# The last three output products by seven block products instead of eight

## The chip, the cores and the metric

The kernel runs on one core of a Trainium2 chip. It uses the core's five engines, which run side by side and meet only at semaphores: TensorE (PE in the profile, with its weight loads as PEld), VectorE (DVE), ScalarE (ACT), GpSimd (POOL) and SyncE (SP). The metric is the device time of one execution in microseconds. Before the change it is 248.94 us, the median of three runs from 248.42 to 251.67.

## The reference

The program is a linear attention followed by a multiplicative feed-forward network (FFN). There are 8 batches, 8 heads, 576 positions and a head width of 64; the FFN has 4608 tokens (all batches and positions), width 512 and inner width 1024.

```python
q_p = phi(q, cos_w, sin_w)                  # max(x, 0) times cos and sin, concatenated: 128 features
k_p = phi(k, cos_w, sin_w)
kv  = einsum('bhsf,bhsd->bhfd', k_p, v)
num = einsum('bhsf,bhfd->bhsd', q_p, kv)
den = einsum('bhsf,bhf->bhs', q_p, sum(k_p, axis=2)) + 1e-06
x   = (num / den) as [4608, 512]            # heads side by side
h   = ((x @ w1) * (x @ w2)) @ w3            # [4608, 1024]
out = h @ w_out                             # [4608, 512], float32
```

The kernel multiplies w3 and w_out together once, into `w34b` (1024 x 512, bf16), so that a token's output is `((x @ w1) * (x @ w2)) @ w34b`.

## The kernel before, in words

The FFN works on nine tiles of 512 tokens (`ffn_groups(t)`, t from 0 to 8). For each of eight blocks `jc` of the inner width it makes two products of four matmuls of 512 columns, `x @ w1` and `x @ w2` (line 655). ScalarE copies the first out of its PSUM bank as `asb` (line 693), and VectorE multiplies it with the second into `abT[:, jc, :]` (line 698), which lies with the inner width on the partitions and the tokens along the row. Then four output products (one for each 128 tokens, `ms`) take eight matmuls of 512 columns each, with a slice of `abT` as the stationary operand and `w34b[:, jc, :]` as the moving one (line 703). ScalarE copies each to an output buffer (line 709). In the last tile the fourth of them is made in two halves of 256 columns (line 720), which ScalarE and VectorE evict (line 722) and SP stores. The FFN's PSUM banks are four, in rotation, so a bank comes back after three further products.

Outputs go in pairs: an output buffer `osb` holds 256 tokens by 512 columns of float32 (0.52 MB). The list `held` has the pairs that are computed and not yet stored; `st` issues the store of the oldest (line 643) from POOL, `sg` does so behind a one-element copy that waits for the newest `asb` (the copy `seen`, line 415), `sx` behind one that waits for the newest transpose. A pair goes out in two to four DMAs of 128 or 256 KB, or one of 512 KB.

Attention feeds the FFN. For batch b and block c of 128 positions (block 4 has 64): `q b c` and `k b c` make the features (lines 491, 495 and 498, on VectorE and ScalarE), `v b c` copies v (line 510, with V, A or G for VectorE, ScalarE or GpSimd), `qd b c` has SP transpose the features of q by DMA into `qpT` (line 518), `kv b` makes the 40 matmuls of k by v (line 539) and the copies `kvs`, `n b c` eight matmuls of `qpT` by `kvs` into a PSUM pair `pnum` (line 571), `d b c` the division on VectorE (lines 582 to 584, the result is `xblk`), and `xd b c` has SP transpose it by DMA into `xT` of its FFN tile (line 604). Tile 7 needs batch 6's blocks 1 to 4 and batch 7's block 4; tile 8 needs batch 7's blocks 0 to 3. `pnum` has two pairs of banks in turn.

The order of the work on every engine is written out by hand: `PLAN` is a text, a line for each step `f t` of an FFN tile (half of a `jc` pair, or half of an output product) with the attention steps, loads and stores that are issued after it. Each engine runs its instructions in that order, and waits only where a semaphore says so. Loads of q, k and v are issued by POOL (`l`, or `lg` and `lt` behind a `seen` copy), in its own order.

Of the kernel before, what the change touches and what calls it, by code (L numbers as in the profile page):

```python
# [81 lines left out]
f 1  # L82
f 1
f 1; qd 2 3; q 3 2; q 3 3; n 2 2
f 1; k 3 4; k 3 2 4; n 2 4; v 3 0 G
f 1; xd 2 0; xd 2 1; d 2 2
f 1
f 1; v 3 4 G; k 3 0; k 3 3 6; k 3 1; q 3 4 6
f 1; n 2 3; qd 3 0; qd 3 3; xd 2 2
f 1; d 2 4; lt 4 k 0; d 2 3  # L90
f 1; kv 3
f 2
f 2; lg 4 q 0
# [102 lines left out]
f 6; qd 7 2  # L196
f 6; d 6 3; qd 7 4; v 7 4 V; q 7 1
f 6; v 7 1 V
f 6
f 6  # L200
f 6; kv 7; qd 7 0; sg
f 6
f 6; xd 6 1; qd 7 3
f 6
f 6; n 7 4
f 6
f 6
f 6; n 7 3; d 7 4
f 6; n 7 2; xd 6 3
f 6; xd 7 4  # L210
f 6
f 7; d 7 3; qd 7 1
f 7
f 7; n 7 0; xd 7 3
f 7; d 7 2
f 7; d 7 0; xd 7 2
f 7; xd 7 0
f 7; n 7 1
f 7
f 7; d 7 1  # L220
f 7; xd 7 1
f 7
f 7; sx
f 7; st
f 7; st
f 7; sg
f 7
f 7; sg
f 7
f 7  # L230
f 7
f 7
f 7
f 7
f 7; st
f 8
f 8
f 8
f 8
f 8; st  # L240
f 8
f 8
f 8
# [12 lines left out]
f 8  # L256
f 8
f 8
f 8; st; st; st; st; st"""
NKP, NVA, NQP, NRQ, NRV, NT3 = 1, 2, 1, 2, 2, 3  # L260


# [49 lines left out]
def kernel(  # L312
# [34 lines left out]
    osbs = [early[:, ds(2048 * i, 2048)].bitcast(FP32).rearrange("p (i m) -> p i m", m=DM) for i in range(6)]  # L347
# [4 lines left out]
    def osb_of(i):  # L352

        return osbs[i % len(osbs)]
# [166 lines left out]
    pairs, taken = [ps_att], [0]  # L521
# [6 lines left out]
    def second_pair():  # L528

        ps_tr_stack.close()  # L530
        pairs.append(ctx.enter_context(tc.tile_pool(name="ps_att2", bufs=1, side="right", reuse_waits="tile",
                                                    space=bass.MemoryType.PSUM)))

    def kv(b):
        a = att_of(b)
# [109 lines left out]
    def ffn_tile():  # L645

        return ffn_pool[0].tile([P, 512], FP32, name="ffnps")

    def ffn_groups(t):
        x = xT[t]  # L650
        abT = fsb.tile([P, 8, 512], BF16, name="abT", bufs=2)

        def products(out, w, jc, tok):
            for kc in range(4):
                nc.tensor.matmul(out, lhsT=w[:, kc, ts(jc, 128)], rhs=x[:, kc, tok],  # L655
                                 start=(kc == 0), stop=(kc == 3))

        def on_half(half):

            for pair in range(2):  # L660
                a, b = ffn_tile(), ffn_tile()
                if pair == 0:
                    for quarter in range(2):
                        for i in range(2):
                            for ps, w in ((a, w1b), (b, w2b)):
                                products(ps[:, ds(256 * i + 128 * quarter, 128)], w, i,
                                         ds(256 * half + 128 * quarter, 128))
                            if half == 0 and quarter == 0 and i == 0:
# [15 lines left out]
                yield  # L684

        if t <= 1:
            yield from on_half(0)
            yield from on_half(1)
        for jc in range(4 if t <= 1 else 0, 8):
            aT = ffn_tile()  # L690
            products(aT[:, :], w1b, jc, slice(0, 512))
            asb = fsb.tile([P, 512], BF16, name="asb")
            nc.scalar.copy(out=asb[:], in_=aT[:, :])  # L693
            newest[0] = asb
            yield
            bT = ffn_tile()
            products(bT[:, :], w2b, jc, slice(0, 512))
            nc.vector.tensor_mul(out=abT[:, jc, :], in0=asb[:], in1=bT[:, :])  # L698
            yield
        for ms in range(3 if t == NT - 1 else 4):  # L700
            ops = ffn_tile()
            for jc in range(8):
                nc.tensor.matmul(ops[:, :], lhsT=abT[:, jc, ts(ms, 128)], rhs=w34b[:, jc, :],  # L703
                                 start=(jc == 0), stop=(jc == 7))
                if jc == 3:
                    yield
            if ms % 2 == 0:
                osb = osb_of(2 * t + ms // 2)
            nc.scalar.copy(out=osb[:, ms % 2, :], in_=ops[:, :])  # L709
            if t == NT - 1:  # L710
                store(nc.sync, osb[:, ms % 2:ms % 2 + 1, :], 4 * t + ms, 1)
            elif ms % 2 == 1:
                held.append((osb, 4 * t + ms - 1))
            yield
        if t == NT - 1:
            for half in range(2):
                cols = ts(half, 256)
                ops = ffn_tile()
                for jc in range(8):
                    nc.tensor.matmul(ops[:, 0:256], lhsT=abT[:, jc, ts(3, 128)],  # L720
                                     rhs=w34b[:, jc, cols], start=(jc == 0), stop=(jc == 7))
                (nc.vector.tensor_copy if half else nc.scalar.copy)(out=osb[:, 1, cols], in_=ops[:, 0:256])
                store((nc.sync, nc.scalar), osb[:, 1:2, :], 4 * t + 3, 1, cols)
                yield

    def store_next():
        osb, g = held.pop(0)
# [54 lines left out]
    def behind_first_x(c):  # L784

        if c in att[0]["x"]:
            gate(att[0]["x"][c][:, 0, 0, 0:1])

    def gated_store():

        gate(newest[0][:, 0:1])
        store_next()

    def store_behind_transposes():
# [13 lines left out]
        "d": norm, "xt": x_tr, "xd": x_dma, "idle": idle_mms, "open": open_ffn, "second": second_pair,  # L808
        "clear": clear_rows, "t3": w3_tr, "st": store_next,
        "sg": gated_store, "sx": store_behind_transposes,  # L810
    }
    for line in PLAN.splitlines():
# [34 lines left out]
```

## Time and profile before

| what | before |
|---|---|
| median of three runs | 248.94 us |
| the profiled execution: span, first to last instruction | 245.8 us |
| around the span (median less span) | 3.1 us |
| TensorE busy | 238.9 us, 1891 matmuls |
| VectorE busy | 147.9 us, 373 instructions |
| ScalarE busy | 118.5 us, 210 instructions |
| GpSimd busy | 88.9 us, 171 instructions |

The page of the profile gives the span of the profiled execution and not its whole time, so the span is compared with the median of the runs. A row of the timeline has the start in the span, the duration, the engine, the line of the kernel, the operation, what it writes and reads, and in brackets how long its engine was idle before it and what ended that. A busy TensorE is not TensorE at its peak, because matmuls are pipelined: what one of them costs is the distance between their starts, not the duration of one.

### The profile page before, as it was taken

How to read it: one execution, taken by the hardware profiler on the slowest of the kernel's cores; microseconds unless marked ns; L12 is line 12 of the kernel's file. 1: busy time of each engine (PE TensorE's matmuls, PEld its weight loads, DVE VectorE, ACT ScalarE, POOL GpSimd, SP SyncE). 2: the span in 40 equal slices, each digit the busy share in tenths (PEclk: the TensorE clock that was granted, in tenths of full speed). 3: DMA queues.
4: the chain of work that ended last, by engine and by line, in shares of the span. 5: the costliest groups of instructions: out<-in, count | busy, mean ns of one | idle time of the engine just before them, and what ended most of it. 6: DMA issues, size and time to landing. Idle time of an engine off the chain costs nothing.

```text
span 245.8 us, 5011 instructions
## 1 busy us (share of the span) xinstructions
PE 238.9 (97%) x1891; PEld 129.9 (53%) x1891; DVE 147.9 (60%) x373; ACT 118.5 (48%) x210; POOL 88.9 (36%) x171
## 2 busy tenths in 40 slices
PE   8899999989999999999999999999999999999994
PEld 3589434567964545445544544454545454444442
DVE  6976558968888546925855576378458327403320
ACT  2834323767756734755466436558343333323321
POOL 8854887534403170006124023024001000497800
PEclk9999999999999999999999999999999999999999
DMA  7999999999999999879999999999337332489933
GB/s 198 195 196 199 195 177 191 199 199 168 165 163 167 182 135 195 129 138 153 193 138 148 168 144 159 234 148 185 75 61 148 96 75 44 68 267 338 302 119 128
DMA packets 84552, 40.44 MB, mean 165 GB/s; under 512 B 48048, under 2 KB 82096, under 8 KB 84528
## 3 DMA queue, kind: packets, MB, share of 16 engines
q0 software_dynamic: 38832, 27.27, 69.3%
q1 hardware_dynamic: 45696, 12.85, 32.6%
q8 instruction: 15, 0.25, 0.4%
q14 instruction: 9, 0.07, 0.1%
HBM read 38.80 MB, written 9.44 MB: 196 GB/s over the span
## 4 chain that ended last, share of the span: by engine, by line
PE 77%; DMA 9%; POOL 6%; DVE 4%; issue 1%; DVEq 0%; POOLq 0%
PE ffnps L655 45%; PE ffnps L703 24%; DMA early<-in_moe_w_out_dram 4%; PE pnum L571 4%; PE pnum L539 3%; POOL early L403 3%; DMA kf<-in_k_dram 3%; DMA q<-in_q_dram 2%; DVE w3T L460 1%; POOL w2b L776 1%; POOL early L409 1%; DVE kp L491 1%; POOL w1b L776 1%; PE ffnps L720 1%; DVE qp L491 1%
## 5 line engine op out<-in xcount | busy, mean ns | idle before, releaser
L698 DVE TENSOR_TENSOR abT<-asb,ffnps 128x512 bf16<-128x512 bf16 x64 | 43.7, 685 | 56.8 <-PE ffnps L655 56.4
L655 PE MATMUL ffnps<-xT,w1b 128*128 128x512 bf16 (+2 forms) x352 | 76.0, 340 | 0.0
L655 PE MATMUL ffnps<-xT,w2b 128*128 128x512 bf16 (+2 forms) x352 | 76.0, 340 | 0.0
L693 ACT CAST asb<-ffnps 128x512 bf16<-128x512 f32 x64 | 37.4, 584 | 58.6 <-PE ffnps L655 45.5
L703 PE MATMUL ffnps<-w34b,abT 128*128 128x512 bf16 x280 | 65.0, 379 | 0.0
L655 PEld LDWEIGHTS <-w1b 128*128 128x128 bf16 x352 | 31.7, 98 | 28.4
L655 PEld LDWEIGHTS <-w2b 128*128 128x128 bf16 x352 | 31.6, 98 | 28.0
L703 PEld LDWEIGHTS <-abT 128*128 128x128 bf16 x280 | 26.2, 98 | 28.9
L584 DVE TENSOR_TENSOR xblk<-pnum,den 128x512 bf16<-128x512 f32 (+1 forms) x39 | 26.9, 691 | 1.5 <-DVE den L583 0.2
L415 POOL COPY seen<-asb 128x1 bf16<-128x1 bf16 x13 | 2.6, 198 | 50.5 <-ACT asb L693 50.4
L495 ACT ACTIVATE kp<-kf,sinv 128x512 bf16<-128x512 bf16 (+4 forms) x33 | 20.7, 656 | 0.3 <-DMA kf<-in_k_dram 0.3
L495 ACT ACTIVATE qp<-qs,sinv 128x512 bf16<-128x512 bf16 (+6 forms) x30 | 18.3, 626 | 1.9 <-DMA qs<-in_q_dram 0.8
L571 PEld LDWEIGHTS <-qpT 128*128 128x128 bf16 x320 | 15.0, 98 | 7.2
L709 ACT COPY early<-ffnps 128x512 f32<-128x512 f32 x19 | 11.1, 585 | 15.4 <-PE ffnps L703 14.2
L571 PE MATMUL pnum<-kvs,qpT 128*128 128x65 bf16 x312 | 15.9, 194 | 0.0
L491 DVE TENSOR_SCALAR kp<-kf,cosv 128x512 bf16<-128x512 bf16 (+1 forms) x40 | 14.4, 379 | 2.1 <-DMA kf<-in_k_dram 2.1
L470 PE MATMUL ffnps<-early,w3T 128*128 128x512 bf16 x64 | 14.5, 379 | 0.5 <-DVE w3T L460 0.5
L415 POOL COPY seen<-xT 128x1 bf16<-128x1 bf16 x6 | 1.2, 193 | 36.6 <-DMA xT<-xblk 36.6
L510 POOL COPY va<-vs 128x512 bf16<-128x512 bf16 (+1 forms) x13 | 8.2, 639 | 13.7 <-DMA vs<-in_v_dram 13.7
L491 DVE TENSOR_SCALAR qp<-qs,cosv 128x512 bf16<-128x512 bf16 (+1 forms) x35 | 12.5, 368 | 0.0
L372 POOL DMA_DIRECT2D vs<-in_v_dram x16 | 10.7, 681 | 2.4 <-PE ffnps L470 1.1
L460 DVE STREAM_TRANSPOSE w3T<-early 128x1024 bf16<-128x1024 bf16 x8 | 9.7, 1231 | 2.5 <-DMA early<-in_moe_w_dram 2.5
(90 smaller groups left out, 225.5 us busy)
## 6 DMA issues: line engine op xcount, KB each, us to landing
kf<-in_k_dram POOLq DMA_DIRECT2D x7, 320.0 KB, 7.5
early<-in_moe_w_dram POOLq DMA_DIRECT2D x16, 128.0 KB, 5.3
out_dram<-osb POOLq DMA_DIRECT2D x8, 256.0 KB, 5.2
qs<-in_q_dram POOLq DMA_DIRECT2D x6, 320.0 KB, 6.6
vs<-in_v_dram POOLq DMA_DIRECT2D x6, 320.0 KB, 8.0
kf<-in_k_dram POOLq DMA_DIRECT2D x7, 256.0 KB, 8.2
qs<-in_q_dram POOLq DMA_DIRECT2D x6, 256.0 KB, 7.9
vs<-in_v_dram POOLq DMA_DIRECT2D x6, 256.0 KB, 9.3
```

Source lines behind the costliest of these rows:

```text
L372: eng.dma_start(out=t[ts(half, 64), :, 0:j, :].rearrange("p h j d -> p h (j d)"), in_=rows[:, span, :].rearrange("h (p j) d -> p h (j d)", ...
L460: nc.vector.transpose(out=w3Ts[jp][:, l0:l0 + n, :].rearrange("p l (c i) -> p l c i", c=4), in_=w3b[:, jp, :].rearrange("p (c l j) -> p l ...
L470: nc.tensor.matmul(acc[:, :], lhsT=w3T[:, lc, :], rhs=woutb[:, lc, :], start=(lc == 0), stop=(lc == 7))
L491: nc.vector.tensor_scalar(out=dst[:R, c, :, 0:D], in0=rows[:R], scalar1=0.0, scalar2=cosv[:R, at:at + 1], op0=ALU.max, op1=ALU.mult)
L495: nc.scalar.activation(out=dst[:R, c, 0:n, D:F], in_=rows[:R, 0:n], func=ACTF.Relu, scale=sinv[:R, at:at + 1], bias=0.0)
L571: nc.tensor.matmul(nt[:, h // 4, ds((h % 4) * 65, 65)], lhsT=qpT[:, h, ds(at, 128)], rhs=kvs[:, h, :], start=True, stop=True)
L584: nc.vector.tensor_tensor(out=xblk[rows, g0:g0 + ng], in0=n4[:, :, :, 0:D], in1=den[rows, 0:ng].unsqueeze(3).to_broadcast([R, ng, 4, D]), ...
L655: nc.tensor.matmul(out, lhsT=w[:, kc, ts(jc, 128)], rhs=x[:, kc, tok], start=(kc == 0), stop=(kc == 3))
L693: nc.scalar.copy(out=asb[:], in_=aT[:, :])
L698: nc.vector.tensor_mul(out=abT[:, jc, :], in0=asb[:], in1=bT[:, :])
L703: nc.tensor.matmul(ops[:, :], lhsT=abT[:, jc, ts(ms, 128)], rhs=w34b[:, jc, :], start=(jc == 0), stop=(jc == 7))
L709: nc.scalar.copy(out=osb[:, ms % 2, :], in_=ops[:, :])
```

## The change

With a 2 x 2 split of everything, a tile's `abT` has the blocks a11, a12, a21, a22 (rows: 256 tokens; columns: 512 of the inner width), `w34b` has b11 to b22 (512 of the inner width by 256 columns), and the output has c11 to c22. Tiles 6, 7 and 8 make the output from seven products of blocks instead of eight, by sums of blocks on both sides (Strassen's scheme in Winograd's form). Four sums of blocks of `w34b` (t1 to t4, called `blocks`) are made once by POOL in tile 1 (`tw`), in the place in `early` that the first two output buffers had; so there are 12 output buffers instead of 14. The sums of a tile's own blocks are made by VectorE as its `jc` go by: s3 = a11 - a21 after jc 3; s1 = a21 + a22, in place, and s2 = a22 - s3 in two halves after jc 5 and jc 7; then s4 = a12 - s2. The products are m1 = a11 b11, m7 = s3 t3, m6 = s2 t2, m5 = s1 t1, m2 = a12 b21, m4 = a22 t4, m3 = s4 b22, in this order, each as eight matmuls of 256 columns. ScalarE copies m1 and m7 out; the rest are additions with a PSUM operand on VectorE and, in two sums (u3 and the last of c22), without one: on VectorE in tile 6 and on POOL in tiles 7 and 8. The tile `abT` has one buffer instead of two.

In the plan, batch 7's steps in tile 6 are moved: `kv 7` is one step earlier, the transposes of q and of batch 6 are drawn together, `n 7 3` and `n 7 2` go into tile 7. Nine `ss` steps stand in tile 7 and three in tile 8. After the last transpose, `more` gives the second pair of `pnum` banks to the FFN. The twelve pairs that POOL stored from tile 7 on are stored by SP (`ss`), without the gates; the last tile's four blocks are stored by SP and ScalarE as they are ready.

```diff
 f 6; v 7 1 V
+f 6; qd 7 3
+f 6; kv 7; qd 7 0; sg
+f 6; qd 7 1
+f 6; n 7 4; xd 6 1
+f 6; d 7 4; xd 6 3
+f 6; xd 7 4
...
+f 7; n 7 3
 f 7
+f 7; d 7 3; n 7 2
+f 7; xd 7 3
+f 7; d 7 2; n 7 0
+f 7; xd 7 2
+f 7; d 7 0; n 7 1
 f 7; xd 7 0
 f 7; d 7 1
 f 7; xd 7 1
+f 7; more
+f 7; ss
...
+f 8; ss
...
+SEVEN = (6, 7, 8)
+ON_POOL, MORE_BANKS = (7, 8,), (7, 8,)
...
+            if seven and jc == 3:
+                sums(abT, s, 0, 4, 3)
+            if seven and jc == 5:
+                sums(abT, s, 0, 2, 2, 1)
+            if seven and jc == 7:
+                sums(abT, s, 2, 2, 2, 1)
+                sums(abT, s, 0, 4, 4)
...
+        m1 = product(A_of(abT, 0, 0), B_of(0, 0), halves=(0,))
+        yield
+        product(A_of(abT, 0, 0), B_of(0, 0), halves=(1,), into=m1)
+        nc.scalar.copy(out=c11, in_=block(m1))
+        yield
+        m7 = product(s3, t3, True)
+        nc.scalar.copy(out=c22, in_=block(m7))
+        yield
+        m6 = product(s2, t2)
+        add(c21, block(m6), c11)
+        yield
+        m5 = product(A_of(abT, 1, 0), t1, True)
+        add(block(u3), c21, c22, side)
+        add(block(u4), block(m5), c21)
+        yield
+        m2 = product(A_of(abT, 0, 1), B_of(1, 0))
+        add(c22, c22, block(u4), side)
+        add(c11, block(m2), c11)
+        out_now(0, 0, nc.sync)
+        out_now(1, 1, nc.scalar)
+        yield
+        m4 = product(A_of(abT, 1, 1), t4, True)
+        add(c21, block(m4), block(u3))
+        out_now(1, 0, nc.sync)
+        yield
+        if last:
+            for ms in range(2):
+                m3 = bank(False)
+                for kc in range(4):
+                    nc.tensor.matmul(m3[:, 0:256], lhsT=s4[:, kc, ts(ms, 128)], rhs=B_of(1, 1)[:, kc, :],
+                                     start=(kc == 0), stop=(kc == 3))
+                add(c12[:, ms, :], m3[:, 0:256], block(u4)[:, ms, :])
+                out_now(0, 1, (nc.sync, nc.scalar)[ms], ms)
...
+    def store_by_sync():
+        osb, g = held.pop(0)
+        store(nc.sync, osb[:, :, :], g, 2)
```

Here `side` is POOL in tiles 7 and 8 and VectorE in tile 6, `product(..., True)` takes one of the further banks where they are open, and `out_now` issues the store of a block in the last tile.

More of the change, by code (lines that the diff above doesn't have):

```diff
@@ L232 @@
 f 7
[L233 to L240, printed above, removed]
+f 8; ss
+f 8; ss
+f 8; ss
 f 8
@@ L346 @@
     w3b = early[:, 4096:12288].rearrange("p (c j) -> p c j", j=DFF)
-    osbs = [early[:, ds(2048 * i, 2048)].bitcast(FP32).rearrange("p (i m) -> p i m", m=DM) for i in range(6)]
+    blocks = [early[:, ds(1024 * i, 1024)].rearrange("p (c m) -> p c m", m=256) for i in range(4)]
+    osbs = [early[:, ds(2048 * i, 2048)].bitcast(FP32).rearrange("p (i m) -> p i m", m=DM) for i in range(2, 6)]
     osbs += [const.tile([P, 2, DM], FP32, name=f"osb{i}") for i in range(MORE - 2)]
@@ L684, in on_half @@
                 yield
+        seven = t in SEVEN
+        s = [fsb.tile([P, 4, 256], BF16, name=f"s{i}", bufs=1) for i in range(3)] if seven else None
         if t <= 1:
+            abT = new_abT()
             yield from on_half(0)
@@ L724, in ffn_groups, with A_of, B_of, weight_block @@
                 yield
+    def A_of(abT, r, c, i0=0, n=4):
+        return abT[:, ds(4 * c + i0, n), ts(r, 256)]
+    def B_of(r, c):
+        return w34b[:, ts(r, 4), ts(c, 256)]
+    def weight_block(i):
+        a, b = ((B_of(0, 1), B_of(0, 0)), (B_of(1, 1), blocks[0]), (B_of(1, 1), B_of(0, 1)), (B_of(1, 0), blocks[1]))[i]
+        nc.gpsimd.tensor_tensor(out=blocks[i], in0=a, in1=b, op=ALU.subtract)
+    def sums(abT, s, i0, n, *which):
+        s3, s2, s4 = (x[:, ds(i0, n)] for x in s)
+        a11, a12, a21, a22 = (A_of(abT, r, c, i0, n) for r in range(2) for c in range(2))
+        for i in which:
+            out, a, b, op = {3: (s3, a11, a21, ALU.subtract), 1: (a21, a21, a22, ALU.add),
+                             2: (s2, a22, s3, ALU.subtract), 4: (s4, a12, s2, ALU.subtract)}[i]
+            nc.vector.tensor_tensor(out=out, in0=a, in1=b, op=op)
```

91 lines of the change are left out of this document (62 added, 29 removed).

## The prediction

> **What bounds the kernel now.** I read the page's totals first, then the chain of waits, then the rows of single lines.
>
> ```profile
> PE 238.9 (97%) x1891; PEld 129.9 (53%) x1891; DVE 147.9 (60%) x373; ACT 118.5 (48%) x210; POOL 88.9 (36%) x171
> PEclk9999999999999999999999999999999999999999
> ```
>
> TensorE is busy for 97% of the span at a full granted clock; no other engine is above 60%. The chain of waits, in order of time, from tile 6 on:
>
> ```profile
> 189.52 1.27 PE pnum L539 x40
> 190.79 1.73 PE ffnps L655 x8
> 192.51 1.73 PE ffnps L703 x8
> ...
> 214.52 6.91 PE ffnps L703 x32
> 221.43 13.81 PE ffnps L655 x64
> 235.24 5.18 PE ffnps L703 x24
> 240.42 1.76 PE ffnps L720 x16
> 242.18 0.02 issue
> 242.20 0.42 DVE early L722
> ```
>
> TensorE is never made to wait in this stretch, so a matmul taken out is time won, unless a new wait eats it. An output product of a tile is 32 matmuls of 512 columns in 6.91 us (0.216 each). After the last matmul (242.18) come one eviction (to 242.62) and the last store; the span ends at 245.8, 3.18 us after that eviction. The span is 245.8 us, the median of the runs 248.94: 3.1 us lie around the span, and I keep them.
>
> **The change, part by part.**
>
> *The products.* Seven block products are 7 x 8 = 56 matmuls of 256 columns instead of 32 of 512. The last tile of before already has that form (L720: all its matmuls and weight loads):
>
> ```profile
> L720 PEld LDWEIGHTS <-abT x16: 97/98/98, 240.0 to 241.8; 128*128 128x128 bf16 x16
> L720 PE MATMUL ffnps<-w34b,abT x16: 272/272/273, 240.3 to 241.9; 128*128 128x256 bf16 x16
> ```
>
> Sixteen took 1.76 us in the chain, 0.110 each with the edge, 0.108 by half of 0.216: the 98 ns weight load still hides behind the 108 ns stream, with little to spare. 56 x 0.108 = 6.05 us, so 0.86 saved in each of tiles 6, 7 and 8: **-2.59 us**, if every operand is there in time.
>
> [...]
>
> *VectorE's sums.* Each tile adds, on VectorE, six bf16 operations SBUF to SBUF: s3 and s4 of 1024 elements, and s2 and s1 in halves of 512. No row has such an operation; the nearest, grouped by shape, are:
>
> ```profile
> L563 DVE COPY qpT<-pst 128x1024 bf16<-128x1024 bf16 x3 | 2.1, 688 | 0.4 <-PE pst L557 0.3
> L460 DVE STREAM_TRANSPOSE w3T<-early 128x1024 bf16<-128x1024 bf16 x8 | 9.7, 1231 | 2.5 <-DMA early<-in_moe_w_dram 2.5
> L563 DVE COPY qpT<-pst 128x512 bf16<-128x512 bf16 x1 | 0.4, 424 | 0.0
> L698 DVE TENSOR_TENSOR abT<-asb,ffnps 128x512 bf16<-128x512 bf16 x64 | 43.7, 685 | 56.8 <-PE ffnps L655 56.4 <-ACT asb L693 0.3
> ```
>
> Two elements a cycle gives 0.69 and 0.42 us, one a cycle 1.23 and 0.69. I take the first (both copy rows are plain bf16 moves) and keep the second. Let T be the end of a tile's last L655 product. The multiply runs from T+0.1 to T+0.8, the second half of s2 to T+1.2, s1 to T+1.6, s4 to T+2.2. The order of products is m1 (a11, ready), m7 (s3, ready since jc 3), m6 (s2, starts T+1.73), m5 (s1, T+2.6), m2, m4, m3 (s4, T+5.2). Even at one element a cycle s2 ends at T+1.5. Cost on TensorE: nothing; m1 and m7 hide it.
>
> *Evictions.* Four 512-wide ScalarE copies become two on ScalarE and up to seven additions, in tile 6 all on VectorE: 7 x 0.65 = 4.6 us (by the L698 row above and what the next instruction overlaps; the SBUF ones put at the same), plus 2.1 of multiply and sums and 1.1 of a normalisation: 7.8 us from T+0.1 on, before the next tile's first multiply at about T+8.0. VectorE trails TensorE by up to 1.7 us. The four banks still hold: m5's bank is read by T+5.1 and wanted at T+6.05, m2's by T+6.5, wanted at T+7.2. Tiles 7 and 8 give two additions to POOL and get two more banks. Nothing, if those rates hold.
>
> *The moved steps of batch 7.* `kv 7` goes one product (0.86 us) earlier, to 188.66. VectorE before it, in order of time:
>
> ```profile
> 186.78 0.16 DVE L582 TENSOR_SCALAR den<-pnum 128x8 f32<-128x8 f32 x1
> 186.97 0.20 DVE L583 RECIPROCAL den<-den 128x8 f32<-128x8 f32 x1
> 187.21 0.69 DVE L584 TENSOR_TENSOR xblk<-pnum,den 128x512 bf16<-128x512 f32 x1
> 187.81 0.27 DVE L510 COPY va<-vs 64x512 bf16<-64x512 bf16 x1
> 188.01 0.34 DVE L491 TENSOR_SCALAR qp<-qs,cosv 128x512 bf16<-128x512 bf16 x1
> 188.28 0.28 DVE L510 COPY va<-vs 128x512 bf16<-128x512 bf16 x1
> ```
>
> s3 now stands in front of these, and VectorE has no gap there, so all slide by 0.65 (1.2): the last copy of va ends at 189.2 (189.75). kv 7 wants that chunk third, 16 matmuls after its start, at 189.17, and the bank that the normalisation in the first three rows (1.1 us) frees. I take **+0.1 us**, bound 0.6.
>
> n 7 4 is also earlier, and d 7 4 is behind the sums: it ends near T+3.3, then SyncE transposes its 64 rows, which tile 7's first product needs at T+6.05. The transposes of xT in this stretch:
>
> ```profile
> L604 SPq DMA_TRANSPOSE xT<-xblk x7: 1172/1190/1298, 186.2 to 209.5; - x7
> DMA to landing us min/median/max: 2.3/2.5/4.2
> ```
>
> 3.3 + 2.5 = T+5.8: on time by 0.25 us. On SP, qd 7 3, qd 7 0 and qd 7 1 now go ahead of xd 6 1 and xd 6 3, which are issued by about 192.7, so the queue is free. I take 0; with sums at one element a cycle it is 0.8 late, with a 4.2 us landing 1.4 late. The other four normalisations lie in tile 7 with ten products behind them. Nothing.
>
> *Weight blocks on POOL.* Four two-input operations of 1024 elements, two ahead of `v 3 4 G`, two ahead of batch 4's gated loads. POOL there, and its nearest row:
>
> ```profile
> 76.11 1.17 POOL L510 COPY va<-vs 128x512 bf16<-128x512 bf16 x2
> 83.96 0.19 POOL L415 COPY seen<-xT 128x1 bf16<-128x1 bf16 x1 [6.68 <-DMA xT<-xblk]
> 84.48 0.68 POOL L372 DMA_DIRECT2D kf<-in_k_dram  x1 [0.33 <-issue]
> 87.20 0.19 POOL L415 COPY seen<-asb 128x1 bf16<-128x1 bf16 x1 [2.04 <-ACT asb L693]
> 87.71 1.35 POOL L372 DMA_DIRECT2D qs<-in_q_dram  x2 [0.33 <-issue]
> ```
> ```profile
> L510 POOL COPY va<-vs 128x512 bf16<-128x512 bf16 x10 | 6.3, 638 | 13.0 <-DMA vs<-in_v_dram 13.0
> ```
>
> At the copy's rate 1.28 us each; reading two inputs one after the other, 2.55. I take the second. Two end at about 81.8 and the va copy at 82.5; kv 3 reads it from 84.14 on (row below), so it is hidden up to 3.4 us each. The other two end at 90.3 instead of 85.2, and q's loads leave 2.8 us later (kv 3 on TensorE, the first use of that q on VectorE, and how q's loads land):
>
> ```profile
> 84.14 1.44 PE L539 MATMUL pnum<-va,kp 128*128 128x65 bf16 x40
> ```
> ```profile
> 96.91 1.04 DVE L491 TENSOR_SCALAR qp<-qs,cosv 128x512 bf16<-128x512 bf16 x2
> ```
> ```profile
> DMA to landing us min/median/max: 6.6/6.8/7.1
> ```
>
> They land by 98.3 instead of 95.5, up to 1.4 us after VectorE's first use. A bank comes round again three products (2.6 us) later, so TensorE would not yet wait. I take 0; bounds 0 and 1.5.
>
> [...]
>
> *The stores.* 12 pairs of 0.52 MB go from SP instead of POOL. SyncE's last transposes in the timeline, the stores' issues (KB each, us to landing), and the stretch in which POOL's stores flow best (the last two columns are DMA share and GB/s):
>
> ```profile
> 198.66 12.11 SPq L604 DMA_TRANSPOSE xT<-xblk  x4
> ```
> ```profile
> out_dram<-osb POOLq DMA_DIRECT2D x8, 256.0 KB, 5.2
> out_dram<-early SPq DMA_DIRECT2D x3, 256.0 KB, 2.4
> out_dram<-early SPq DMA_DIRECT2D x2, 128.0 KB, 2.0
> ```
> ```profile
> 226.00:229.00 3.00, 3.00 (x15) 1.37 (x14) 1.25 (x2) 0.99 (x2) 2.37 (x5) 1.00 0.99 335
> ```
>
> They start behind xd 7 1, near 210.5 as before. 6.3 MB at 335 GB/s take 19 us, to about 230, clear of the last tile's. Nothing.
>
> *The end.* T of tile 8 is 235.24 - 1.73 + 0.1 = 233.6; its last matmul ends at 239.65, and the last addition (two 256-wide ones after c21) at T+6.6 = 240.2 against 242.62: **-2.4 us**. But before, the last 128 KB store left almost alone; now c22, c21 and the two halves of c12, 0.79 MB, leave within 0.75 us from 239.6. One 256 KB store lands in 2.4 us and the other 0.52 MB at 335 GB/s add 1.6: 243.6, against 242.3 for the last store alone. The cost is 0 to 1.3; I take **+0.6**.
>
> **Sum:** -2.59 + 0.10 + 0.06 (the last addition stands 0.06 later behind TensorE) + 0.6 = -1.8 us. The span becomes 244.0, the time 248.94 - 1.8 = **247.1 us**.
>
> **The rivals.**
>
> 1. *A new wait replaces the gain.* Sums at one element a cycle: kv 7 0.6, xT of tile 7 0.8, the stores 1.3: -2.59 + 2.76 = +0.2, 249.1. For it: slacks of 0.25 us. Against: the copy rows.
> 2. *Slower: SP's stores don't drain.* The last tile's stores stand in SP's queue behind 6.3 MB. If that queue runs slower than POOL's, they wait. All 7.34 MB must be out by about 243.3, from 210.5: it decides below 224 GB/s. At 195 GB/s the last byte leaves at 248.1, 4.8 later: 251.9; at 165, 258.8. For it: no row shows an SP store with others in flight. Against: 256 KB land in 2.4 us from SP, 5.2 from POOL, and eight may be in flight.
> 3. *POOL holds batch 3 or 4 up.* At 4 us a block, va is 1.2 late for kv 3 and q's loads are 5.8 late: some 1 to 3 us, 248 to 250.
> 4. *The change doesn't shorten the products.* At 0.115 (the 98 ns load nearly on the path) 56 cost 6.44, and 0.47 a tile is saved: 248.3.
> 5. *Weight loads not hidden:* 24 x 0.098 - 0.86 = +1.5 a tile, 248.9 + 4.5 + 0.7 for the end: 254.1. The L720 rows speak against it. [...]
>
> **How the numbers follow.** Forecast (246.2 to 248.2) 0.66; rival 1 0.13; rival 2 0.07; rival 3 0.08; rival 4 0.04; rival 5 0.01; 0.01 for more than all of it. From 245.9, where stores at the end and kv 7 cost nothing and 0.5 comes on top, to 249.6, which takes in rivals 1, 4 and most of 3, no more than 2 in 10 is left out. Two per cent, 5 us, is about what a measurement of this kernel tells from no change (its runs range over 3.2 us). Slower by that takes rival 2 at under about 187 GB/s, rival 5, or the far end of rival 3: 0.07. Faster by that would need twice the matmuls saved: 0.03. Within: 0.90.
>
> **What would show it.** Right: the block products (line 794 of the changed kernel) at 0.108 a matmul with no gap; less than 0.3 us between tile 6's last product and tile 7's first; kv 7 within 0.3 of its place; DMA quiet from about 231; the last store landing 2 to 3 us after the last addition. Wrong: gaps on TensorE at kv 3, kv 7 or tile 7's start, 256-column matmuls above 0.115, or output still draining when the last addition ends.

## The result and the profile after

The changed kernel takes **252.05 us** (median of four runs, 251.59 to 253.44), the kernel before 248.68 us in the runs beside it and before (247.87 to 251.67). The ratio is 1.0155, 95% interval 1.012 to 1.019. By the 2% bound that is no change, but the forecast was 247.1 us and the range ended at 249.6: the sign was wrong, and the time lies 5.0 us over the forecast. Two of the experiments' profiles, of `e3_both` and `e5_tile7_pool`, are of disturbed executions; those two are read by their times alone.

The page of after, its span and the row of engines:

```profile
span 250.2 us, 5192 instructions
...
PE 237.8 (95%) x1955; PEld 135.9 (54%) x1955; DVE 168.4 (67%) x408; ACT 115.1 (46%) x204; POOL 85.8 (34%) x142
```

TensorE does 1.1 us less than before (238.9), VectorE 20.5 us more, and the span is 4.4 us longer than the 245.8 of before. The part that was to be shortened was shortened. The chain of waits of after, in order of time (start, duration, engine, tile, line):

```profile
190.54 0.28 DVE va L513
190.82 0.05 issue
190.87 1.45 PE pnum L548 x40
...
195.16 6.11 PE ffnps L794 x56
201.27 0.86 PE ffnps L667 x4
...
222.23 13.81 PE ffnps L667 x64
236.04 0.87 PE ffnps L794 x8
...
241.33 0.04 issue
241.38 1.02 DVE osb L802 x2
```

The 56 block matmuls of tile 6 take 6.11 us (0.109 each) and tile 7's first product follows without a gap, at 201.27. Three tiles take 18.33 us instead of 20.76: 2.43 us won. So 6.8 us were lost elsewhere, nearly all of it at three places: the end, batch 3 and the start. VectorE's sums of `abT` blocks (line 774) cost what had been taken for them:

```profile
230.04 0.69 DVE L774 TENSOR_TENSOR s<-abT 128x1024 bf16<-128x1024 bf16 x1
...
236.87 0.42 DVE L774 TENSOR_TENSOR s<-abT,s 128x512 bf16<-128x512 bf16 x1
```

**At the end.** In the timeline of after, SyncE's stores up to the end of tile 7's output (SPq), VectorE's last additions, and the last tile's stores by ScalarE (ACTq) and SyncE:

```profile
229.64 15.36 SPq L652 DMA_DIRECT2D out_dram<-early  x12
...
241.99 0.75 DVE L802 TENSOR_TENSOR osb<-ffnps,s 128x256 f32<-128x256 f32 x2
242.25 0.94 ACTq L652 DMA_DIRECT2D out_dram<-osb  x2
245.10 1.63 SPq L652 DMA_DIRECT2D out_dram<-osb  x3
```

The last addition ends at 242.74, the span at 250.2: 7.46 us, against 3.18 before. c11 was ready at 241.2, and SyncE issued nothing of the last tile before 245.10. The waits view of SyncE (waited for: us in total, times, longest), and four stretches (us, then busy time of PE, PEld, DVE, ACT and POOL, granted clock, DMA share, GB/s):

```profile
SPq L652 <- DMA out_dram<-osb: 7.2, 1, 7.2
```
```profile
229.00:238.00 9.00, 9.00 (x53) 5.00 (x52) 6.02 (x11) 3.10 (x6) 0.00 (x0) 1.00 0.88 257
238.00:240.00 2.00, 2.00 (x21) 1.80 (x19) 1.35 (x3) 0.41 (x1) 0.41 (x1) 1.00 0.22 84
240.00:242.00 2.00, 2.00 (x20) 1.69 (x18) 1.58 (x4) 0.00 (x0) 1.92 (x2) 1.00 0.00 0
242.00:245.00 3.00, 0.16 (x2) 0.00 (x0) 0.73 (x3) 0.00 (x0) 0.21 (x1) 1.00 0.39 131
```

SyncE waits 7.2 us for one store of a block of the last tile, and within that wait the DMA engines move nothing at all for 2 us (0 GB/s from 240 to 242). So it is not a queue that drains slowly: the bytes issued so far were out, and the next store was not issued. Which store it waits for is seen in the compiled program of after, in SyncE's list (and, as its last line here, one entry of ScalarE's) with the semaphores that each entry waits for:

```
81 L652 DMACopy out_dram<-q0f 64x512 [waits DMAHW1_49]
...
88 L652 DMACopy out_dram<-early 64x512 [waits DMAHW0_49]
89 L652 DMACopy out_dram<-early 64x512 [waits DMAHW2_49]
...
94 L652 DMACopy out_dram<-early 64x512 [waits DMAHW0_49]
95 L652 DMACopy out_dram<-early 64x512 [waits DMAHW1_49]
96 L652 DMACopy out_dram<-osb_82 128x2x256 [waits DMAHW2_49,DVE_49]
...
166 L652 DMACopy out_dram<-osb_83 128x2x256 [waits DMAHW1_49,Pool_49]
```

The stores of SyncE and ScalarE share eight semaphores in turn: in the trace of after SyncE's 99 DMAs carry DMAHW0 to DMAHW7, 12 or 13 times each, and ScalarE's two carry two of the same, DMAHW1 and DMAHW4. Each waits until the last user of its own is done. Between SyncE's 88th and 89th entry the turn of DMAHW1 went to ScalarE's 166th: the store of c22 in the last tile. SyncE's 95th, the last piece of tile 7's output, is the next user. It was ready long before, but it waits for c22, which ScalarE issues at 242.25 and which lands 2.3 us later, at 244.5; and c11, c21 and half of c12 stand behind it in SyncE's queue. It was SyncE that stood, for 7.2 us, and the DMA engines had nothing to move in two of them.

**In batch 3.** The timelines of TensorE around kv 1 and kv 3, after and then before (kv 3 of before, at 84.14, stands in the prediction):

```profile
68.77 1.44 PE L548 MATMUL pnum<-va,kp 128*128 128x65 bf16 x40
83.62 0.43 PE L580 MATMUL pnum<-kvs,qpT 128*128 128x65 bf16 x8 [0.30 <-DVE xblk L593]
86.23 1.44 PE L548 MATMUL pnum<-va,kp 128*128 128x65 bf16 x40 [0.46 <-POOL seen L418]
```
```profile
67.78 1.43 PE L539 MATMUL pnum<-va,kp 128*128 128x65 bf16 x40
```

From kv 1 to kv 3 it is 17.46 us, 1.10 more than the 16.36 of before, and TensorE waits where it did not. In that stretch, GpSimd and VectorE in the timeline of after, the view of VectorE's line 494 of after (ns, least, median and most), and VectorE in the timeline of before:

```profile
76.98 2.12 POOL L765 TENSOR_TENSOR early<-w34b 128x1024 bf16<-128x1024 bf16 x1
79.18 2.12 POOL L765 TENSOR_TENSOR early<-w34b,early 128x1024 bf16<-128x1024 bf16 x1
81.24 0.67 POOL L513 COPY va<-vs 64x512 bf16<-64x512 bf16 x1
```
```profile
77.73 0.69 DVE L714 TENSOR_TENSOR abT<-asb,ffnps 128x512 bf16<-128x512 bf16 x1 [0.76 <-PE ffnps L667]
78.34 3.11 DVE L494 TENSOR_SCALAR qp<-qs,cosv 128x512 bf16<-128x512 bf16 x2
81.37 0.95 DVE L494 TENSOR_SCALAR kp<-kf,cosv 64x512 bf16<-64x512 bf16 x2
```
```profile
L494 DVE TENSOR_SCALAR qp<-qs,cosv x2: 920/1596/2272, 78.3 to 79.2; 128x512 bf16<-128x512 bf16 x2
```
```profile
77.34 0.69 DVE L491 TENSOR_SCALAR qp<-qs,cosv 128x512 bf16<-128x512 bf16 x2
```

GpSimd's copy of va is done at 81.9, over 4 us before kv 3: that is not what kv 3 waits for. Its row names GpSimd's one-element copy `seen` as the last event before it, but that is beside the point: in after, `e1_sp_only`, `e5a_tile7_pool_only` and `e8_quarters` alike, kv 3 starts 0.15 us behind the end of a division on VectorE (line 593, here from 85.39 to 86.08). But the two feature operations of VectorE take 0.92 and 2.27 us instead of 0.35 each, and they end (79.3 and 81.5) just behind the ends of GpSimd's two weight blocks (79.10 and 81.30). While a block ran, VectorE's bf16 operation from SBUF did not get on, and the divisions behind it, which free `pnum`, were late.

**At the start.** kv 1 stands at 68.77 instead of 67.78, 0.99 later, behind steps that are the same in both plans.

**At kv 7.** TensorE in the timelines of after and then before:

```profile
190.87 1.45 PE L548 MATMUL pnum<-va,kp 128*128 128x65 bf16 x40
```
```profile
189.35 1.43 PE L539 MATMUL pnum<-va,kp 128*128 128x65 bf16 x40
```

From kv 5 to kv 7 it is 52.03 us (138.84 to 190.87), before 52.60 (136.75 to 189.35). One product of 0.86 us fewer stands between them, so 51.74 would be on time: kv 7 is 0.29 us late.

The sum, of the two profiles: 0.99 at the start, 1.10 in batch 3, 0.29 at kv 7, -2.43 for the products, 0.17 to the last addition, 4.28 behind it: 4.4 us. The medians differ by 3.4 us and the ratio is 1.55% (3.9 us). In every run on record the time is 1.7 to 2.1 us above the span, so the profiled execution of before (245.8) took about 247.8 us, less than the median of 248.68: some 0.5 to 1 us of the 4.4 is a difference between executions, and not the change.

### The profile page after: what moved, and what is told of

Same layout as the page of the kernel before. It is cut to its first block, busy times and chain, and to the rows that moved or that the text cites. A ratio compares the mean times of both kernels' runs of the same rounds, so it can differ in the third digit from the quotient of the medians.

```text
span 250.2 us, 5192 instructions
## 1 busy us (share of the span) xinstructions
PE 237.8 (95%) x1955; PEld 135.9 (54%) x1955; DVE 168.4 (67%) x408; ACT 115.1 (46%) x204; POOL 85.8 (34%) x142
## 4 chain that ended last, share of the span: by engine, by line
PE 66%; DMA 15%; POOL 7%; DVE 5%; issue 3%; SPq 0%; ACT 0%; DVEq 0%; POOLq 0%
PE ffnps L667 39%; PE ffnps L729 13%; PE ffnps L794 5%; DMA w2b<-in_moe_w_dram 4%; DMA qpT<-qp 4%; PE pnum L548 3%; PE pnum L580 3%; DMA kf<-in_k_dram 3%; PE ffnmore L794 2%; DMA q<-in_q_dram 2%; DMA early<-in_moe_w_dram 2%; POOL early L765 2%; POOL w2b L897 1%; POOL early L406 1%; POOL w1b L897 1%
## 5 line engine op out<-in xcount | busy, mean ns | idle before, releaser
L729 PE MATMUL ffnps<-w34b,abT 128*128 128x512 bf16 x192 | 45.0, 379 | 0.0
L729 PEld LDWEIGHTS <-abT 128*128 128x128 bf16 x192 | 17.8, 98 | 19.2
L494 DVE TENSOR_SCALAR qp<-qs,cosv 128x512 bf16<-128x512 bf16 (+1 forms) x35 | 15.4, 453 | 0.0
L548 PE MATMUL pnum<-va,kp 128*128 128x65 bf16 x280 | 10.4, 194 | 1.3 <-DVE kp L501 0.6
L456 PE MATMUL unread<-zeros 128*128 128x512 bf16 x31 | 10.4, 485 | 1.2 <-DVE zeros L433 1.2
L548 PEld LDWEIGHTS <-kp 128*128 128x128 bf16 x280 | 9.8, 97 | 3.2 <-issue 1.1
```

The costliest lines, as they stand in the source:

```text
L494: nc.vector.tensor_scalar(out=dst[:R, c, :, 0:D], in0=rows[:R], scalar1=0.0, scalar2=cosv[:R, at:at + 1], op0=ALU.max, op1=ALU.mult)
L548: nc.tensor.matmul(kvt[:, h // 4, ds((h % 4) * 65, 65)], lhsT=a["kp"][:, c, h, :], rhs=a["va"][:, c, h, 0:D + 1], start=(i == 0 and h % 4 ...
```

## The experiments

The theory: two things cost the time, SyncE's wait for ScalarE's store at the end and GpSimd's hold on VectorE in batch 3. The rivals: that stores by SyncE, or two engines that store at once, are slow in themselves; that GpSimd's queue (va, the loads) is what is late; that the moved steps or VectorE's sums cost something.

One table holds what all runs measured: the ratio to the kernel before (times beside it on the same chip), the distance from kv 1 to kv 3 on TensorE, and the time from the end of the last addition or eviction to the end of the span. All of these kernels compute the whole result.

| run | median us | ratio [95%] | kv 1 to kv 3 | behind the last addition |
|---|---|---|---|---|
| before | 248.1 to 248.7 | 1 | 16.36 | 3.18 |
| after | 252.05 | 1.0155 [1.012, 1.019] | 17.46 | 7.46 |
| e1_sp_only | 249.67 | 1.0062 [1.0032, 1.0092] | 18.38 | 4.54 |
| e2_blocks_dve | 250.61 | 1.0103 [1.0071, 1.0136] | 16.37 | 7.2 |
| e3_both | 247.79 | 0.9994 [0.996, 1.0028] | not read | not read |
| e4_eight | 249.51 | 1.0071 [1.0051, 1.009] | 18.13 | 3.0 |
| e5a_tile7_pool_only | 249.04 | 1.0028 [1.0006, 1.005] | 17.99 | 4.2 |
| e5_tile7_pool | 248.42 | 0.9981 [0.9955, 1.0008] | not read | not read |
| e6_tail | 248.41 | 1.0007 [0.9986, 1.0027] | 16.37 | 4.2 |
| e7_s3_late | 247.75 | 0.9957 [0.9924, 0.999] | 16.38 | 4.13 |
| e8_quarters | 250.93 | 1.0113 [1.0091, 1.0134] | 16.86 | 7.2 |
| e9_before_again | 247.78 | one run | 16.37 | 3.2 |
| e10_moves_only | 248.15 | 1.0009 [0.9988, 1.003] | 16.38 | 2.9 |
| e12_pool_c22 | 247.82 | 0.998 [0.9958, 1.0003] | 16.70 | 4.57 |

### e1_sp_only: no store by ScalarE at the end

```diff
-        out_now(1, 1, nc.scalar)
...
         out_now(1, 0, nc.sync)
+        out_now(1, 1, nc.sync)
...
-                out_now(0, 1, (nc.sync, nc.scalar)[ms], ms)
+                out_now(0, 1, nc.sync, ms)
```

> All five stores of the last tile by SP, none by ScalarE; everything else as after. Theory A (SP's queue stood from 237.3 to 244.5 behind the wait of tile 7's last store for the semaphore that it shares with ScalarE's store of c22): the wait is gone, the last store leaves within 1 us of the last addition, and 3.5 to 5 us are won: 247 to 248.5 us. Rival B (SP's queue is simply slow, 0.6 to 0.7 us an issue, and is still behind at the end): the two further stores on SP make it no faster, 252 to 253 us.

SyncE in the timeline of this run, and two stretches in the same columns as above:

```profile
230.42 8.42 SPq L652 DMA_DIRECT2D out_dram<-early  x12
241.70 2.87 SPq L652 DMA_DIRECT2D out_dram<-osb  x5
```
```profile
240.00:243.00 3.00, 2.69 (x25) 2.15 (x23) 2.47 (x5) 0.00 (x0) 2.54 (x2) 1.00 0.14 47
243.00:246.00 3.00, 0.00 (x0) 0.00 (x0) 0.26 (x1) 0.00 (x0) 0.00 (x0) 1.00 0.93 308
```

Tile 7's stores are issued by 238.8, where after needed until 245.0 for the same twelve, and the last tile's five leave as they are ready. The wait of 7.2 us is gone, and the time falls by 0.9% of before's, 2.4 us, less than the 3.5 to 5 that were expected. In this profile kv 3 stands 18.38 us behind kv 1, 0.92 more than in after, so the blocks on GpSimd took back part of the gain. Behind the last addition it is still 4.54 us, 1.4 over before: there the DMA engines are busy for 0.93 of the time (308 GB/s from 243 to 246), so this part is the pile of the last tile's five stores, and not a wait of SyncE.

### e2_blocks_dve and e3_both: the weight blocks by VectorE

```diff
-f 1; k 3 4; k 3 2 4; n 2 4; v 3 0 G; tw 0
-f 1; xd 2 0; xd 2 1; d 2 2; tw 1
+f 1; k 3 4; k 3 2 4; n 2 4; v 3 0 G
+f 1; xd 2 0; xd 2 1; d 2 2
...
-f 1; d 2 4; lt 4 k 0; d 2 3; tw 2; tw 3
+f 1; d 2 4; lt 4 k 0; d 2 3
...
-f 2
-f 2; qd 4 0
+f 2; tw 0; tw 1
+f 2; qd 4 0; tw 2; tw 3
...
-        nc.gpsimd.tensor_tensor(out=blocks[i], in0=a, in1=b, op=ALU.subtract)
+        nc.vector.tensor_tensor(out=blocks[i], in0=a, in1=b, op=ALU.subtract)
```

> The four sums of weight blocks by VectorE at the end of tile 2 instead of by POOL in tile 1; everything else as after. Theory A (the two 2.1 us operations of POOL hold VectorE's feature operations up, one of which lasts 3 us, and kv 3 comes 1.1 us late): kv 3 keeps its distance from tile 1's products as before, and 0.8 to 1.4 us are won: about 251. Rival B (kv 3 is late because POOL's copy of va comes behind the sums): the same gain, but VectorE's operations would be as long as in after. Rival C (the 1 us is part of the start-up, which varies): no gain, 252.

VectorE in the timeline, the same operation in batch 3, and a block in its new place:

```profile
77.81 0.61 DVE L494 TENSOR_SCALAR qp<-qs,cosv 128x512 bf16<-128x512 bf16 x2
...
104.98 0.68 DVE L765 TENSOR_TENSOR early<-w34b 128x1024 bf16<-128x1024 bf16 x1
```

The two feature operations take 0.61 us again and kv 3 is back at 16.37 us behind kv 1, with no wait of TensorE between. The end stays as in after (7.2 us), and the ratio falls by 0.5%. A block takes 0.68 us on VectorE, a third of GpSimd's 2.12.

`e3_both` has the edits of `e1_sp_only` and of this run together.

> Both edits together. If the two costs are separate and both as read from the trace, they add: 252.05 - 4.4 - 1.1, 246 to 247.5 us, faster than before by 1.5 to 2.5 us. If the end was covering for the middle, less.

0.9994: the two edits together take back the whole loss, 1.6%, about what they do one by one (0.9 and 0.5). But the time is that of before, and not the 1.5 to 2.5 us below it that were expected: what is left, the pile at the end above all (1.4 us in `e1_sp_only`), eats the saving on the products.

### e4_eight: all of the change but the seven products

```diff
-SEVEN = (6, 7, 8)
+SEVEN = ()
```

> Eight products in all tiles, as before, evicted and (in the last tile) stored by SP as before; the moved steps, the sums of weight blocks on POOL (which nothing uses) and SP's stores as after. Theory A: the products' gain of 2.4 us is missing, the cost of POOL's sums of 1.1 us is there, the end is as before: 249.5 to 250.5 us. Rival B (SP's stores in themselves delay the end): 252 or more.

TensorE's one large wait in the timeline of this run, and VectorE at that time:

```profile
78.47 0.81 PE L729 MATMUL ffnps<-w34b,abT 128*128 128x512 bf16 x3 [1.61 <-DVE abT L714]
```
```profile
75.10 2.72 DVE L501 TENSOR_SCALAR qp<-qs,sinv 128x256 bf16<-128x256 bf16 x1
```

The blocks are still made, though nothing reads them here, and this time it is another operation (0.28 us in before) that takes 2.72 us. kv 3 is 1.8 us late, and the 0.7% over before is there without the seven products; `e10_moves_only`, below, has no blocks and loses it. SyncE stores the last tiles here too, and the span ends 3.0 us behind the last eviction, where before it was 3.18: storing by SyncE cost nothing in itself.

### e5a_tile7_pool_only and e5_tile7_pool: tile 7's two pairs by GpSimd

```diff
 f 8; ss
-f 8; ss
-f 8; ss
+f 8; st
+f 8; st
```

> After with one thing changed: tile 7's two pairs are stored by POOL instead of SyncE. The weight blocks stay on POOL in batch 3, and ScalarE still issues two of the last tile's stores. Theory (SyncE's queue stood still because one of tile 7's stores waited for a semaphore that a store of ScalarE's had before it): the wait of 7.2 us is gone, the span ends 4.2 to 4.6 us after the last addition instead of 7.5, and the time falls by about 2.9, to 249.2 (ratio 1.001 to 1.005). Rival (two engines storing at once at the end is slow in itself): 251.5 or more.

This is the clean test of the first cause: ScalarE still stores c22 and half of c12, but nothing of tile 7 stands in SyncE's queue behind its semaphore. SyncE and ScalarE in the timeline of `e5a_tile7_pool_only`, and the row of TensorE that the weight blocks on GpSimd leave:

```profile
241.64 1.84 SPq L652 DMA_DIRECT2D out_dram<-osb  x3
...
242.72 0.94 ACTq L652 DMA_DIRECT2D out_dram<-osb  x2
```
```profile
84.09 0.43 PE L580 MATMUL pnum<-kvs,qpT 128*128 128x65 bf16 x8 [0.82 <-DVE xblk L593]
```

c11 leaves at 241.64, just as its addition ends, and the span ends 4.2 us behind the last addition. From 1.0155 to 1.0028: the wait cost 1.3% of the time, about 3.2 us. Two engines that stored at once were not slow in themselves (with SyncE alone, in `e1_sp_only`, it was 4.54 us). `e5_tile7_pool` has the edit of `e2_blocks_dve` besides.

> The weight blocks by VectorE at the end of tile 2, and tile 7's two pairs stored by POOL; the last tile's stores by SP and ScalarE as in after. Theory A (what held SP was the semaphore shared by tile 7's last store and ScalarE's store of c22): no store of SP is now behind one of ScalarE, so the end is short although ScalarE still stores: 1 us less than with both earlier edits, 246 to 247.5 us. Rival B (any store of ScalarE's beside SP's delays the end): 249.5 to 251, like the blocks on VectorE alone.

0.9981, another 0.5% (1.2 us) less: the second cause, by its time. At 248.42 us it is not the 246 to 247.5 that were expected of it, nor less than `e3_both`.

### e8_quarters: each weight block in four pieces

```diff
-        nc.gpsimd.tensor_tensor(out=blocks[i], in0=a, in1=b, op=ALU.subtract)
+        for c in range(4):
+            nc.gpsimd.tensor_tensor(out=blocks[i][:, c], in0=a[:, c], in1=b[:, c], op=ALU.subtract)
```

> After, with each of POOL's four sums of weight blocks in four pieces of 256 elements. Theory A (each POOL operation holds VectorE's bf16 feature operations up for as long as it runs, and they go ahead between two of them): VectorE's longest wait falls from 2 to 3 us to under 1, the sum of POOL's time is somewhat longer, kv 3 is late by 0 to 0.8 us: 251 to 252 us. Rival B (VectorE is slowed all the same while POOL works): kv 3 late by 1 us or more, 252 to 252.6.

GpSimd in the timeline, a whole block and then the copy of va:

```profile
77.39 2.71 POOL L766 TENSOR_TENSOR early<-w34b 128x256 bf16<-128x256 bf16 x4
80.06 2.64 POOL L766 TENSOR_TENSOR early<-w34b,early 128x256 bf16<-128x256 bf16 x4
82.66 0.66 POOL L513 COPY va<-vs 64x512 bf16<-64x512 bf16 x1
```

The blocks take longer in all (2.7 instead of 2.1 us each), and va is later than in after (83.3 instead of 81.9), yet kv 1 to kv 3 is 16.86 us, 0.6 less than in after. If GpSimd's queue had been what kv 3 waited for, it would have been more. VectorE got in between the pieces: its two feature operations (line 494, at 78.34) take 1.23 us together, where after had 3.11.

### e6_tail, e7_s3_late and e12_pool_c22: what is left

`e6_tail` takes `e5_tile7_pool` and puts c22's last sum on VectorE, with the last stores in turn on SyncE and ScalarE; `e7_s3_late` also makes s3 behind product 5 instead of 3; `e12_pool_c22` takes `e5_tile7_pool` with s3 late, and leaves c22 on GpSimd.

```diff
-            if seven and jc == 3:
-                sums(abT, s, 0, 4, 3)
             if seven and jc == 5:
+                sums(abT, s, 0, 4, 3)
                 sums(abT, s, 0, 2, 2, 1)
...
-        add(c22, c22, block(u4), side)
+        add(c22, c22, block(u4), nc.vector if last else side)
+        out_now(1, 1, nc.sync)
         add(c11, block(m2), c11)
-        out_now(0, 0, nc.sync)
-        out_now(1, 1, nc.scalar)
+        out_now(0, 0, nc.scalar)
...
-                out_now(0, 1, (nc.sync, nc.scalar)[ms], ms)
+                out_now(0, 1, (nc.scalar, nc.sync)[ms], ms)
```

> As the run before it, and in the last tile c22's last sum by VectorE instead of POOL, so that it is stored 1.4 us earlier, and the five stores alternate between SP and ScalarE. Theory A (0.79 MB in the last 0.75 us costs 1.3 us behind the last addition): 0.5 to 1 us less, 245.5 to 247 us. Rival B (the fixed landing time alone sets the end): the same time or 0.3 more, for VectorE's longer chain.

> As the run before it, and s3 made after jc 5 instead of jc 3, so that it doesn't stand in front of the va copy and the division that kv 7 waits for. Theory A (the 0.3 us gap before kv 7 is VectorE's delay by s3): the gap goes, 0.2 to 0.4 us less, 245 to 246.8 us, faster than before by 0.6 to 1.2%. Rival B: the gap stays, as the transposes or the k features set it.

> The version of e7_s3_late (blocks on VectorE at the end of tile 2, tile 7's pairs by POOL, s3 behind product 5), but the tail of the last tile is that of after: c22's last sum on POOL and its store by ScalarE. In e7_s3_late the last addition ends 7.30 us after the start of tile 8's last multiply, in after 6.59, because c22's sum stands on VectorE and waits 0.63 us for POOL. Theory (the last addition sets the end, about 4.2 us behind it): 0.7 us less than e7_s3_late, a ratio of 0.993. Rival (the pile of 0.79 MB sets the end, and c22's store, which leaves 2.3 us later here, makes the pile longer): the same as e7_s3_late, 0.996, with the span ending 4.6 us or more after the last addition.

The tail of `e7_s3_late` and then that of `e12_pool_c22`, VectorE's last multiply, a sum and the last additions:

```profile
234.47 0.69 DVE L714 TENSOR_TENSOR abT<-asb,ffnps 128x512 bf16<-128x512 bf16 x1 [0.77 <-PE ffnps L667]
...
239.21 0.69 DVE L801 TENSOR_TENSOR osb<-osb,s 128x512 f32<-128x512 f32 x1 [0.63 <-POOL s L801]
...
241.02 0.75 DVE L801 TENSOR_TENSOR osb<-ffnps,s 128x256 f32<-128x256 f32 x2
```
```profile
234.15 0.69 DVE L714 TENSOR_TENSOR abT<-asb,ffnps 128x512 bf16<-128x512 bf16 x1 [0.77 <-PE ffnps L667]
...
239.99 0.74 DVE L801 TENSOR_TENSOR osb<-ffnps,s 128x256 f32<-128x256 f32 x2
```

In `e7_s3_late` VectorE waits 0.63 us for GpSimd's u3, and its last addition ends 7.30 us after the start of the last multiply; without that, in `e12_pool_c22`, 6.58 us. But the span ends 4.13 us behind it in the first and 4.57 in the second, so 0.44 of the 0.72 us are given back: the store of c22 leaves 1.84 us before the last addition ends in `e7_s3_late` (at 239.93), and 0.48 us before it in `e12_pool_c22` (at 240.25). The times of the two kernels don't tell which tail is better, but the 0.993 that the theory asked of `e12_pool_c22` lies outside its interval. `e6_tail`, which has the same tail as `e7_s3_late`, shows no gain over `e5_tile7_pool`: at 248.41 us the 0.5 to 1 us that were expected of it did not come. Between `e6_tail` and `e7_s3_late` the medians differ by 0.66 us and the intervals touch. The profiles show part of it: kv 7 starts 1.15 us behind the start of the product before it in `e6_tail` and 0.86 in `e7_s3_late`, so making s3 later takes away the whole delay of kv 7, 0.29 us. The rest of the 0.66 is not shown.

`e12_pool_c22` has the blocks on VectorE, and kv 1 to kv 3 is still 0.34 us longer than in before. VectorE and GpSimd in its timeline show why:

```profile
74.56 1.65 DVE L501 TENSOR_SCALAR qp<-qs,sinv 128x256 bf16<-128x256 bf16 x1
```
```profile
74.95 1.17 POOL L513 COPY va<-vs 128x512 bf16<-128x512 bf16 x2
```

The feature operation of 0.28 us takes 1.65 and ends at 76.2, just behind two plain copies by GpSimd (to 76.12), and TensorE waits for the multiplication behind it. The same copies stand in the kernel before; there they ran from 76.11 to 77.28 and met a multiplication with a PSUM operand (line 698, at 76.74), which kept its 0.69 us. So here VectorE was held up beside plain copies as well (1.65 us instead of 0.28), and what they meet differs between profiles. Whether the load that GpSimd issued just before them (to 74.95) had a part in it is open.

None of the three came as low as was expected (245.5 to 247, 245 to 246.8, and 0.993). `e7_s3_late`, at 0.9957 [0.9924, 0.999], is the one version whose interval lies below the kernel before.

### e9_before_again and e10_moves_only: two controls

`e9_before_again` is the kernel before, unchanged.

> The kernel before, unchanged, profiled a second time. The profile of after has kv 1 at 68.77 us and that of before at 67.78, although no instruction ahead of it differs. If that is how one execution differs from another (the medians of before, 248.3 to 248.7, are 0.5 to 0.9 us over the 247.8 of its profiled execution), kv 1 stands between 68.0 and 68.8 here, and the first PE wait at 51 us is near 0.6. If it belongs to the change, kv 1 stands at 67.8 again.

TensorE in its timeline:

```profile
50.66 2.03 PE L539 MATMUL pnum<-va,kp 128*128 128x65 bf16 x40 [0.76 <-POOL va L510]
67.96 1.44 PE L539 MATMUL pnum<-va,kp 128*128 128x65 bf16 x40
```

kv 1 stands at 67.96, a hair below what was expected of the run-to-run theory. In the readable profiles of the changed kernels it stands between 67.83 (`e12_pool_c22`) and 68.89 (`e10_moves_only`), so the same code spreads over 1 us; but that two profiles of before both lie at the low end leaves open whether some tenths of the 0.99 belong to the change.

`e10_moves_only` has eight products, no weight blocks, and tile 7's pairs on GpSimd: of the change, the moved steps of batch 7, SyncE's stores for the other tiles and the fewer buffers are left.

```diff
-SEVEN = (6, 7, 8)
+SEVEN = ()
...
-f 1; k 3 4; k 3 2 4; n 2 4; v 3 0 G; tw 0
-f 1; xd 2 0; xd 2 1; d 2 2; tw 1
+f 1; k 3 4; k 3 2 4; n 2 4; v 3 0 G
+f 1; xd 2 0; xd 2 1; d 2 2
...
 f 8; ss
-f 8; ss
-f 8; ss
+f 8; st
+f 8; st
```

> After with eight products, no weight blocks at all, and tile 7's two pairs stored by POOL: only the moved steps of the last batch and SyncE's stores for the other tiles are left of the change. Theory (the moved steps and SyncE's stores cost nothing by themselves; the 1.0071 of the run with eight products was POOL's lock on VectorE): 1.000, at most 1.003, with no wait of TensorE over 0.3 us between 60 us and the end. Rival (the moved steps or SyncE's stores cost something too): 1.005 or more, with a wait at kv 7 or at the last tile.

1.0009, and no wait of TensorE between 60 us and the end: these parts cost nothing, within 0.3%. The interval also bounds what the start can have cost (0.3%, 0.7 us), and in this profile kv 1 stands as late as 68.89.

## Why the prediction was wrong, step by step

- **The products: right.** -2.43 us against -2.59, at 0.109 us a matmul. Rivals 4 and 5 fall with it: the weight loads are hidden, since a 98 ns load and a 108 ns stream take 109 ns together.
- **VectorE's sums: right.** 0.69 us for 1024 elements and 0.42 for 512, as taken from the copy rows; no row shows the cycles that the prediction calls these times by. The evictions held: the products follow one another without a gap. Rival 1 falls.
- **kv 7: right in kind, too small.** 0.29 us late against 0.1, within the bound of 0.6. It is really VectorE that ends last there (the row of va, line 513, in the chain). But the sum took kv 7's start from the chain, 189.52, where the timeline of before has 189.35, and it looked at the last copy of va; TensorE waits for the copy of 64 rows, which slid by the same 0.65. **xT of tile 7: right**, no wait at 201.27.
- **The weight blocks on POOL: wrong.** The term was 0, bounds 0 and 1.5. In the four profiles with whole blocks on POOL kv 3 is 1.10, 1.63, 1.77 and 2.02 us late (after, `e5a_tile7_pool_only`, `e4_eight`, `e1_sp_only`); by the times, taking the blocks away wins 0.5 to 0.7%, 1.2 to 1.7 us. So even the bound was too low, and the mechanism was not in the prediction: where the number came near it, that was luck. The price of a block was taken as 2.55 us and is 2.12, less. The step that failed is the sentence on who waits: it looked at what stands behind the blocks in POOL's own queue (va, the loads of q), found slack there, and rightly so, since the later loads cost nothing. It did not look at VectorE, which worked from SBUF at the same time and was held up (3.11 us in after for two operations that took 0.69 in before). Rival 3 named a loss in batch 3, but by POOL's own queue at 4 us a block.
- What in the chip holds VectorE up is not shown; the traces show when it was held. In after its two operations, 0.35 us each in before, ended 0.16 and 0.15 us behind the ends of GpSimd's two 2.12 us blocks (79.26 and 81.45 against 79.10 and 81.30), and in `e8_quarters`, beside pieces of 0.7 us, the two were done in 1.23 us together; an operation of VectorE that reads PSUM (0.69 us at 77.73, while the first block ran) was not slowed. In the trace neither of the two waits for a semaphore of GpSimd's, so the two engines did not meet only at semaphores.
- **The stores: slower than taken, but that was not the cost.** SyncE's stores begin at 213.0, not 210.5, and flow at 239 GB/s to 229 and 257 to 238, not at 335 to 230. That is over the 224 GB/s at which rival 2 begins, and by 240 all of them that had been issued were out. Rival 2's time, 251.9, is near the measured one, but its mechanism, a queue without the bandwidth, did not occur: from 240 to 242 us the DMA engines stood idle (share 0.00).
- **The end: wrong.** The term was +0.6, at most 1.3, for stores that leave together; it is +4.28. About 3.2 us of that are the wait of SyncE on a semaphore that ScalarE's later store has before it, which no line of the diff and no row of before shows, because before only SP and POOL stored there, and in its trace SP's DMAs carry DMAHW0 to DMAHW7 and POOL's eight others, DMASW0 to DMASW7. The list of the compiled kernel has it. The prediction priced each queue as if the engine that issues were free whenever its data are ready. The pile itself cost 1.0 to 1.4 us in the runs without the wait, at or just over the far bound of what was taken.
- **Around the span: misread.** The 3.1 us are the median less the span of an execution that was shorter than the median; with time and span of the same run it is 2.1 at most. The forecast adds its changes to the median, so this did not move it.
- **The sum.** With both causes gone, the versions reach 0.9957 to 1.0007, about -1.1 to +0.2 us, against the forecast -1.8: the pile is 0.4 to 0.8 us dearer than taken, kv 7 and the products 0.2 each, and the rest is within what these runs tell apart. How much the start adds stays open, up to some tenths of a microsecond.

## What to carry to other kernels

When a store or load is given to another engine, look at which semaphore it gets and who has it next: if two in-order queues share semaphores in turn, an early DMA of the one can wait for a late DMA of the other, and everything behind it waits too (7.2 us here). When work is put on GpSimd because its queue has room, price also what VectorE does from SBUF meanwhile, since here a 2 us operation, and in one run two plain copies, held 0.3 us operations up to their end; on VectorE the same work took a third of the time (0.68 us a block instead of 2.12). And price the end of a kernel by the last addition, the pile of bytes that leaves together and the state of the queue that they leave by, each by itself.

## What the runs showed of the hardware that was not expected

- VectorE's bf16 feature operation from SBUF took 0.28 to 0.35 us in before, 2.27 us in after and 2.72 in `e4_eight` while GpSimd added two SBUF operands, and 1.65 us in `e12_pool_c22` beside two GpSimd copies; a multiplication on VectorE with a PSUM operand kept its 0.69 us (after, at 77.73).
- A two-input bf16 operation of 128 x 1024 took 2.12 us on GpSimd (after) and 0.68 on VectorE (`e2_blocks_dve`). In four pieces it took 2.5 to 2.7 on GpSimd (`e8_quarters`).
- Stores from SyncE flowed at 257 GB/s over 9 us in after (229 to 238); GpSimd's reached 335 over its best 3 us in before (226 to 229).
- Five stores of 1.05 MB in all (four blocks of 256 KB), issued within 2.9 us at the end, took the DMA engines to 308 GB/s (`e1_sp_only`, 243 to 246) and ended the span 4.1 to 4.6 us behind the last addition in the runs without the wait, where one last store of 128 KB ended it 3.2 us behind in before.
